# Reordering the head of a fused attention and GLU kernel: one load on ScalarE's queue, PSUM copies on ScalarE, late statistics on VectorE, and a GLU block moved ahead

## The chip, the cores and the metric

One core of a Trainium2 chip. The metric is the device time in microseconds. The profile of one execution gives the span from the first to the last instruction, about 1.7 us less than the time. The kernel before was timed on several chips beside the others; its medians there lie between 313.5 and 314.3 us, so each experiment is set against the runs of before on its own chip.

Six terms used throughout: a *block* is 128 rows of x (0 to 3 in the head), a *V half* is 320 of the 640 columns of V, *landing* is the moment the last of a load's 16 semaphore updates is recorded, the *q start* is the start of the first matmul of the q projection (everything before it is the *head*), the *chain* is the chain of waits that ended last, and the *granted clock* is the share of TensorE's full clock that the profile records. In the profile lines L600 is line 600 of that run's kernel. A chain line gives start, length, engine, tile and line; a timeline line gives start, busy time, engine, line, operation and tile, and in brackets how long the engine was idle before it and what ended that.

## The reference, cut to what matters

```python
xn = layernorm(x)                                    # x: 2048 x 640, bf16
qkv = xn @ wqkv                                      # 32 heads of 20, causal window of 256
a = softmax(mask(q @ k.T * 20 ** -0.5)) @ v @ wo
h = sigmoid(xn @ w_gate) * (xn @ w_up)               # 640 -> 1536
out = x + a + h @ w_down
```

## The kernel before: the parts that matter

The head loads x in four row blocks and V's weights in two halves, normalises each block, transposes it on TensorE and forms V before q and k. Engines run their instructions in the order in which they stand here.

```python
load_rows(0, nc.sync); load_rows(1, nc.sync)
load_v(0)                                            # first V half
load_rows(3, nc.sync); load_rows(2, nc.sync)
load_v(1)                                            # second V half
load_wqkv(0); load_wqkv(1)                           # q, k
...
for n in (6, 4):                                     # ten warming matmuls, 128x512 of ones
...
mv0 = ln_block(0, 0)                                 # VectorE: statistics of block 0
xn1, neg1 = mean_act(1)                              # ScalarE: mean of block 1
r0 = root(mv0)                                       # ScalarE: square root for block 0
r1 = root_act(1, xn1, neg1)                          # ScalarE: variance and root of block 1
norm(0, mv0, r0)                                     # VectorE
for lo, hi in ((0, 3), (3, DC)):
    transpose_rows(0, dve, lo, hi)                   # TensorE, then a copy out of PSUM
v00 = project_v(0, 0, 0)                             # TensorE: block 0, first V half
... # block 1, block 3 (its statistics on ScalarE), block 2
```

Much later the out projection of chunk 2 holds two PSUM banks open, and a GLU block of chunk 3 runs between its down sums and its wo sums:

```python
def g_out(c, between):
    for s in range(SBC):
        rows = new_rows(c, s)
        ys = [ps_d.tile([P, CW], FP32, name=f"y{i}", tag="d") for i in range(2)]
        for y, cut in zip(ys, HALVES):
            yield from down(c, s, y, cut)
        if s == 0:
            yield from between                       # one GLU block, two more banks
        outp(c, s, ys, rows)
```

The softmax here doesn't subtract the row's maximum and nothing guards it: scores larger than these inputs give would overflow.

## Time and profile before

| | before |
|---|---|
| time | 313.46 us median of 6 (313.23 to 315.04) |
| span of the profiled run | 311.6 us |
| TensorE busy | 304.0 us |
| first transposes on TensorE | 5.39 us |
| q start | 13.48 us |
| landings: block 1, first V half, block 3, block 2, second V half | 3.60, 5.90, 6.33, 6.78, 8.37 us |

TensorE is the bound, so the table is read by its first real work and by the q start. One profile is one execution: in another profile with the same head (e3) the second V half landed at 9.96 us and q started at 14.65, so differences of a microsecond between single profiles are not read as effects unless the waits in them show the cause. Landings are read from the semaphore records in the trace. The lines of the page and of the chain are shown in the prediction.

### The profile page before, as it was taken

The page shows a single profiled execution, that of the slowest core. Times are in us where ns is not written, and L with a number is a line of the kernel's source. Part 1 is how long each engine was busy: PE and PEld are TensorE (multiplying, and loading weights), DVE is VectorE, ACT ScalarE, POOL GpSimd, SP SyncE. Part 2 cuts the span into 40 slices and gives each one's busy share as a digit, 9 for nine tenths or more (in the row PEclk, how much of TensorE's full clock was granted, in tenths as well). Part 3 has the DMA queues.
Part 4 walks back from the last instruction along what each step waited for, and adds up shares of the span by engine and source line. Part 5 has one row for each costly group of instructions (what it writes and reads, how often), then busy time and mean ns, then how long its engine had stood idle before and what let it go on. Part 6 is the DMA issues. An engine that isn't in the chain of part 4 may idle for free.

```text
span 311.6 us, 10512 instructions
## 1 busy us (share of the span) xinstructions
PE 304.0 (98%) x4627; PEld 175.3 (56%) x4663; DVE 159.5 (51%) x314; ACT 192.4 (62%) x178; POOL 155.5 (50%) x239
## 2 busy tenths in 40 slices
PE   7999999999999999999999999999999999999996
PEld 2654444556557655644567665744556675444774
DVE  4633656639696164388826154362723526272523
ACT  6613878697763747787673647768585547778000
POOL 3000675676782828567382627546372845556000
PEclk9999999999999999999999999999999999999999
DMA  7995999574633153620025213730000223000002
GB/s 219 374 358 173 313 381 189 192 188 159 190 80 95 44 158 113 207 96 2 2 44 86 87 57 92 231 109 2 2 3 2 69 62 109 0 4 0 2 23 65
DMA packets 37614, 35.71 MB, mean 115 GB/s; under 512 B 10272, under 2 KB 37024, under 8 KB 37536
## 3 DMA queue, kind: packets, MB, share of 16 engines
q1 hardware_dynamic: 37280, 34.92, 37.8%
q8 instruction: 36, 0.59, 0.8%
q10 hardware_dynamic: 288, 0.11, 0.1%
q14 instruction: 10, 0.08, 0.1%
HBM read 23.63 MB, written 10.26 MB: 109 GB/s over the span
## 4 chain that ended last, share of the span: by engine, by line
PE 96%; issue 1%; DVE 1%; DMA 1%; ACT 0%; SPq 0%; DVEq 0%
PE y L421 17%; PE pu L407 17%; PE pg L400 17%; PE pqk L294 14%; PE ps L471 9%; PE pv L321 7%; PE y L428 7%; PE acc L503 7%; DMA xc<-in_A_x_dram 1%; PE pt L274 0%; DVE xnT L275 0%; ACT xn L598 0%; DVE h L411 0%; DVE xn L267 0%; SPq L171 0%
## 5 line engine op out<-in xcount | busy, mean ns | idle before, releaser
L479 POOL TENSOR_SCALAR_AFFINE_SELECT pT<-pT 128x512 bf16<-128x512 bf16 (+2 forms) x192 | 147.0, 796 | 129.2 <-ACT pT L476 129.1
L476 ACT ACTIVATE pT<-ps 128x2048 bf16<-128x2048 f32 x76 | 142.7, 1878 | 63.9 <-PE ps L471 59.2
L411 DVE SCALAR_TENSOR_TENSOR h<-th,pu 128x512 bf16<-128x512 f32 x48 | 32.7, 683 | 60.9 <-PE pu L407 49.2
L407 PE MATMUL pu<-xnT,wu 128*128 128x512 bf16 x228 | 59.2, 380 | 0.7
L400 PE MATMUL pg<-xnT,wg 128*128 128x512 bf16 x225 | 57.8, 380 | 1.0 <-issue 0.5
L421 PE MATMUL y<-wd,h 128*128 128x320 bf16 (+2 forms) x396 | 57.0, 296 | 0.0
L294 PE MATMUL pqk<-xnT,wqkv 128*128 128x512 bf16 x191 | 45.5, 381 | 0.5
L421 PEld LDWEIGHTS <-h 128*128 128x128 bf16 x396 | 36.5, 98 | 14.3
L403 ACT ACTIVATE th<-pg 128x512 f32<-128x512 f32 x48 | 28.6, 595 | 14.5 <-PE pg L400 14.0
L400 PEld LDWEIGHTS <-wg 128*128 128x128 bf16 x240 | 22.3, 98 | 25.3 <-issue 0.2
L407 PEld LDWEIGHTS <-wu 128*128 128x128 bf16 x240 | 21.9, 98 | 25.4 <-issue 0.6
L471 PEld LDWEIGHTS <-kT 20*64 20x64 bf16 x1856 | 20.6, 103 | 24.5 <-issue 22.6
L471 PE MATMUL ps<-qT,kT 20*64 20x128 bf16 (+4 forms) x1856 | 32.7, 239 | 0.1
L294 PEld LDWEIGHTS <-wqkv 128*128 128x128 bf16 x200 | 22.6, 119 | 18.0 <-issue 0.6
L432 DVE SCALAR_TENSOR_TENSOR rows<-y,rows 128x320 bf16<-128x320 f32 x30 | 14.5, 490 | 33.2 <-PE y L428 30.0
L513 DVE STREAM_TRANSPOSE t<-acc 128x512 f32<-128x512 f32 x32 | 22.0, 710 | 18.5 <-PE acc L503 18.2
L525 DVE TENSOR_TENSOR on<-t,rec 128x320 bf16<-128x320 f32 (+4 forms) x48 | 27.5, 573 | 1.1
L321 PE MATMUL pv<-wqkv,xnT 128*128 128x320 bf16 x160 | 23.6, 300 | 0.9 <-DVE xnT L275 0.9
L428 PE MATMUL y<-wo,oc 128*128 128x320 bf16 (+2 forms) x165 | 24.2, 295 | 0.0
L503 PE MATMUL acc<-pT,v 128*32 128x64 bf16 (+3 forms) x1376 | 23.2, 223 | 0.1
L503 PEld LDWEIGHTS <-v 128*32 128x32 bf16 x1376 | 18.6, 97 | 7.9 <-issue 1.9
L321 PEld LDWEIGHTS <-xnT 128*128 128x128 bf16 x160 | 14.9, 98 | 7.3 <-DVE xnT L275 1.3
(44 smaller groups left out, 132.6 us busy)
## 6 DMA issues: line engine op xcount, KB each, us to landing
qT<-sq SPq DMA_DIRECT2D x7, 512.0 KB, 5.6
sq<-st SPq DMA_DIRECT2D x20, 128.0 KB, 4.1
sk<-st SPq DMA_DIRECT2D x20, 128.0 KB, 3.0
rows<-in_A_x_dram SPq DMA_DIRECT2D x15, 160.0 KB, 2.4
out_dram<-rows SPq DMA_DIRECT2D x15, 160.0 KB, 1.8
kT<-sk SPq DMA_DIRECT2D x4, 512.0 KB, 6.1
wg<-in_B_w_gate_dram SPq DMA_DIRECT2D x2, 960.0 KB, 7.8
wu<-in_B_w_up_dram SPq DMA_DIRECT2D x2, 960.0 KB, 9.9
```

Of the source, the lines that this page charges most:

```text
L294: nc.tensor.matmul(ps, lhsT=wt[:, m, :], rhs=xnT[c][:, d, :], start=(d == 0), stop=(d == DC - 1))
L321: nc.tensor.matmul(ps[:, 0:HALF], lhsT=xnT[c][:, d, s * P:(s + 1) * P], rhs=wqkv[:, d, 2 * D + hf * HALF:2 * D + (hf + 1) * HALF], start=( ...
L400: nc.tensor.matmul(pg, lhsT=part(wg, d, f), rhs=xnT[c][:, d, :], start=(d == 0), stop=(d == DC - 1))
L403: nc.scalar.activation(out=th, in_=pg, func=TANH, scale=0.5)
L407: nc.tensor.matmul(pu, lhsT=part(wu, d, f), rhs=xnT[c][:, d, :], start=(d == 0), stop=(d == DC - 1))
L411: nc.vector.scalar_tensor_tensor(out=h, in0=th, scalar=1.0, in1=pu, op0=ADD, op1=MULT)
L421: nc.tensor.matmul(y[:, 0:cut[1] - cut[0]], lhsT=ht[c, f][:, s * P:(s + 1) * P], rhs=wd[:, f, cut[0]:cut[1]], start=(f == 0), stop=False)
L428: nc.tensor.matmul(y[:, 0:cut[1] - cut[0]], lhsT=oc[c, m][:, s * P:(s + 1) * P], rhs=wo[:, m, cut[0]:cut[1]], start=False, stop=(m == DC - 1))
L471: nc.tensor.matmul(ps[hf * U:(hf + 1) * U, i, col * U:(col + n) * U], lhsT=qk["k", kc, g // GH][32 * i:32 * i + DH, g % GH, key:key + U], ...
L476: nc.scalar.activation(out=pt[:, :, 0:CW], in_=ps, func=EXP, scale=SCALE)
L479: nc.gpsimd.affine_select(out=out, in_=in_, pattern=[[0, HG], [0, n], [sign, width]], compare_op=GE, fill=0.0, base=base, channel_multipli ...
L503: nc.tensor.matmul(acc[32 * i:32 * i + 32, q * U:(q + n) * U], lhsT=v[:, h * VW:h * VW + 32], rhs=pt[:, i, col * U:(col + n) * U], start=( ...
```

## The change

The second V half goes to ScalarE's queue, so that block 0 can form both V sums one after the other. The copies of blocks 0, 1 and 3 out of PSUM move to ScalarE, the statistics of block 3 to VectorE, the other order follows from that. The GLU block moves ahead of the down sums.

```diff
+    scr = const.tile([P, 1], FP32, name="scr")
+    nc.scalar.activation(out=scr, in_=nc.const_aps.tensor(1.0, [P, 1], FP32), func=SQRT)
-    load_v(1)
+    load_v(1, nc.scalar)
...
-            ys = [...]
+            if s == 0:
+                yield from ahead
+            ys = [...]
...
-    for lo, hi in ((0, 3), (3, DC)):
-        transpose_rows(0, dve, lo, hi)
-    v00 = project_v(0, 0, 0)
+    transpose_rows(0, act)
     norm_act(1, xn1, neg1, r1)
-    xn3, neg3 = mean_act(3)
-    r3 = root_act(3, xn3, neg3)
-    transpose_rows(1, dve)
+    transpose_rows(1, act)
+    v00 = project_v(0, 0, 0)
+    mv3 = ln_block(0, 3)
+    v01 = project_v(0, 0, 1)
+    r3 = root(mv3)
+    v10 = project_v(0, 1, 0)
+    norm(3, mv3, r3)
...  # block 3's copy on ScalarE, block 2's on VectorE, V copies in turns
-    fill.add("out2", g_out(2, g_gu(3, 0, 1)), OUT + GU)
+    fill.add("out2", g_out(2, (), g_gu(3, 0, 1)), OUT + GU)
```

More of the change, by code (lines that the diff above doesn't have):

```diff
@@ L171, in load_rows, with load_v @@
         queue.dma_start(out=xc[0][:, s, :], in_=xr[:, s, :])
-    def load_v(hf):
+    def load_v(hf, queue):
         a = 2 * D + hf * HALF
-        nc.sync.dma_start(out=wqkv[:, :, a:a + HALF], in_=wqkv_r[:, :, a:a + HALF])
+        queue.dma_start(out=wqkv[:, :, a:a + HALF], in_=wqkv_r[:, :, a:a + HALF])
     load_rows(0, nc.sync)
     load_rows(1, nc.sync)
-    load_v(0)
+    load_v(0, nc.sync)
     load_rows(3, nc.sync)
     load_rows(2, nc.sync)
-    load_v(1)
+    scr = const.tile([P, 1], FP32, name="scr")
+    nc.scalar.activation(out=scr, in_=nc.const_aps.tensor(1.0, [P, 1], FP32), func=SQRT)
+    load_v(1, nc.scalar)
     load_wqkv(0)
@@ L232 @@
     nc.gpsimd.memset(eps, EPS)
-    scr = const.tile([P, 1], FP32, name="scr")
-    nc.scalar.activation(out=scr, in_=eps, func=SQRT)
     for n in (6, 4):
@@ L450, in outp, with g_out @@
         store(c, s, rows)
-    def g_out(c, between):
+    def g_out(c, between, ahead=()):
         for s in range(SBC):
             rows = new_rows(c, s)
+            if s == 0:
+                yield from ahead
             ys = [ps_d.tile([P, CW], FP32, name=f"y{i}", tag="d") for i in range(2)]
@@ L621 @@
     norm(0, mv0, r0)
-    for lo, hi in ((0, 3), (3, DC)):
-        transpose_rows(0, dve, lo, hi)
+    transpose_rows(0, act)
+    norm_act(1, xn1, neg1, r1)
+    transpose_rows(1, act)
     v00 = project_v(0, 0, 0)
-    norm_act(1, xn1, neg1, r1)
-    xn3, neg3 = mean_act(3)
-    r3 = root_act(3, xn3, neg3)
-    transpose_rows(1, dve)
+    mv3 = ln_block(0, 3)
[3 more added lines that the diff above has]
+    norm(3, mv3, r3)
+    copy_v(0, 0, 0, v00, act)
     mv2 = ln_block(0, 2)
-    v10 = project_v(0, 1, 0)
-    copy_v(0, 0, 0, v00, act)
+    copy_v(0, 0, 1, v01, act)
+    transpose_rows(3, act)
+    v11 = project_v(0, 1, 1)
     r2 = root(mv2)
-    v01 = project_v(0, 0, 1)
-    norm_act(3, xn3, neg3, r3)
+    copy_v(0, 1, 0, v10, dve)
     norm(2, mv2, r2)
-    copy_v(0, 1, 0, v10, act)
-    transpose_rows(3, dve)
-    v11 = project_v(0, 1, 1)
-    copy_v(0, 0, 1, v01, act)
+    v30 = project_v(0, 3, 0)
+    copy_v(0, 1, 1, v11, act)
     transpose_rows(2, dve)
-    copy_v(0, 1, 1, v11, act)
-    proj_v(0, 3, 0, act)
-    proj_v(0, 3, 1, dve)
+    v31 = project_v(0, 3, 1)
+    copy_v(0, 3, 0, v30, act)
+    copy_v(0, 3, 1, v31, dve)
     proj_v(0, 2, 0, act)
```

## The prediction

> **What bounds the kernel now.** I read the page first, then the chain of waits, then the chain again for two short windows (the head, and the place where the GLU block moves), then the timeline of the head on all engines. From the page:
>
> ```profile
> PE 304.0 (98%) x4627; PEld 175.3 (56%) x4663; DVE 159.5 (51%) x314; ACT 192.4 (62%) x178; POOL 155.5 (50%) x239
> ...
> PE 96%; issue 1%; DVE 1%; DMA 1%; ACT 0%; SPq 0%; DVEq 0%
> ```
>
> The first line is busy time by engine over a span of 311.6 us, the second is the chain that ended last. TensorE is busy for 304.0 us and makes up 96% of the chain: nothing but TensorE's own idle time is left to save, 7.6 us in all. So I looked for where it idles. A list of its gaps from the trace shows only three over 0.2 us after the first matmul (0.51, 0.34, 0.59 us), all before 8 us. The rest are gaps of some 50 ns (single matmul records that are missing) and the time before the first and after the last matmul. The change works on the head, so here is the chain of waits for the first 16 us (start, length, what):
>
> ```profile
> 1.25 2.35 DMA xc<-in_A_x_dram
> ...
> 4.88 0.46 DVE xn L267
> 5.34 0.04 issue
> 5.39 0.36 PE pt L274 x3
> 5.74 0.02 issue
> 5.77 0.37 DVE xnT L275
> 6.13 0.05 issue
> 6.18 0.85 PE pv L321 x5
> 7.03 0.36 PE pt L274 x5
> 7.40 0.02 issue
> 7.42 0.50 DVE xnT L275
> 7.92 0.04 issue
> 7.97 1.53 PE pv L321 x10
> ```
>
> The path goes from one block's norm to its transposes on TensorE (L274), the copy out of PSUM (L275), its V matmuls (L321), then the next block's transposes and copy. From 9.5 us on it is TensorE alone. The projection of q starts at 13.48 us (timeline) and from there the chain is TensorE to the end, so **the start of the first q matmul, 13.48 us, is the figure through which the head moves the total**. From 5.39 to 13.48 us are 8.09 us. One V half is 5 matmuls, 0.136 us apart (2.72 us for 20 in the chain), so 0.68 us; five transposes issue in 0.28 us where they follow at once (10.48 to 10.76 us). 8 x 0.68 + 4 x 0.28 = 6.56 us of work, hence 1.53 us of waiting: that is all that the head's reordering can win.
>
> The second place, around 238 us:
>
> ```profile
> 236.95 1.09 PE pu L407 x5
> 238.05 0.03 issue
> 238.07 0.02 DVEq L411
> 238.09 0.04 issue
> 238.14 0.70 DVE h L411
> 238.84 0.04 issue
> 238.88 0.85 PE acc L503 x47
> ```
>
> Here a VectorE instruction is on the chain. PSUM has four banks in this pool; two hold the open sums y of the out block, two the GLU block's gate and up; the P.V sums of two groups then need two. The first takes the gate's, free early; the second waits until VectorE has read the up bank (h, 238.14 to 238.84).
>
> **What the Trainium skill says.** (1) "DMA: Bandwidth & Descriptors", Issuing engines are not separate DMA queues: loads begun by different engines run on the same 16 DMA engines and interleave; and Queues, rings and completion order: each engine takes turns between queues with work. This trace has only one loading queue in the head, so it can't show the turns; that the DMA engines are full it does show (share 0.61 before 5.39 us, about 1 from there to 24 us, in the windows). (2) "ScalarE: Activation LUTs", What ACT_TABLE_LOAD costs: 1283 ns for a table load (the trace: 1283), an ACTIVATE with immediates 186 + 0.833 ns per element (the trace: 736 ns at 640, the formula 719). (3) "VectorE: DVE Perf Modes", Why PSUM operands drop a tier: a PSUM source caps VectorE at two elements a cycle for bf16. The trace's copy of 128x640 took 492 ns; 640 elements at one per 0.96 GHz cycle would be 667 ns, so it agrees. (4) "TensorE: Matmul & The Clock Gate", What's actually happening: about 3.4 us of work opens the clock, an idle window of about 3.4 us closes it. The warming matmuls' weights are loaded 0.43 us apart, later 512-column matmuls run 0.215 us apart (50 from 13.48 to 24.22 us), which agrees; a pause under 1 us should not close it.
>
> **The change part by part, head.**
> - Start of ScalarE. Table load 0.80 to 2.08 us as before; the small square root no longer waits for GpSimd's eps (0.71 us idle now), so 2.28; the V load's issue, estimated 0.36 us as ScalarE's stores at the end take (0.34 and 0.37), ends at 2.65. Its first real work starts at 3.62 when row block 1 lands: hidden, costs nothing.
> - SyncE issues one load fewer (0.43 us), so q's and k's weights are asked for 0.45 us earlier. They land at 10.65 and 12.90 us (landings in the trace), needed from 13.48: hidden.
> - Copy of block 0 to xnT: VectorE did it in pieces of 357 and 280 ns, the first alone held up the V matmuls. Now one ScalarE copy: by ScalarE's own casts, 422 ns at 320 columns and 580 ns at 512, 0.82 ns each, estimated 0.69 us at 640. It runs 5.88 to 6.57, so xnT of block 0 is later by 0.24 us than its second piece was (6.33).
> - VectorE, freed of it, takes block 1's reciprocal at 5.82 and its norm until 6.46 (now until 6.88). TensorE does block 1's transposes 6.51 to 6.79, then three V sums without a break to 8.83, if V's halves are there. Copy 1 is done by 7.7, before it is needed at 8.15.
> - Statistics of blocks 3 and 2 on VectorE (0.88 + 0.21 us each, then a 0.29 us root on ScalarE, 0.15 reciprocal, 0.45 norm). With block 3 landed (6.33 us now) by 6.49: aggregate done 7.6, root 8.0, norm 8.65, transposes at 8.83 in time. ScalarE copies V00 and V01, then block 3's xnT 9.31 to 10.0; V11 runs to 9.79, V30 waits until 10.05 (0.26 us). Block 2's root comes after that copy in ScalarE's order: 10.29, norm 10.93, transposes at 10.98 (0.25 us waited), V31, then V20 at 12.0 after VectorE's copy, V21 to 13.37.
>
> So if every load comes in time q starts at about 13.4 us, **0.1 us earlier**: the waiting merely moves (0.84 us before block 1's transposes, 0.26, 0.25, 0.07).
>
> - The loads. V's second half is now asked for at 2.3 instead of 3.24 us and takes turns with the first half. The landings are now: first half 5.90, block 3 6.33, block 2 6.78, second half 8.37 us. The 0.4 MB of the second half took about 1.6 us after block 2. Moved ahead of the blocks it can delay both by up to that, and the first half too: with even turns both halves would land near 7.1, block 3 at 7.5, block 2 at 7.9. V00 then starts at 7.1 instead of 6.79, and block 3's statistics at 7.55 instead of 6.49. The same count gives block 3's transposes at 9.65, block 2's at 11.92, V21's end at 14.3: **0.8 us later**.
>
> **GLU block ahead.** The instruction order shows the ten gate and up matmuls moved before the first down sum and nothing else moved; the P.V sums now come after 24 down matmuls, with two banks long free. The first group's P.V starts at 237.96 and takes about 0.68 us, so the second could start at 238.64 and starts at 238.88: **0.24 us saved**.
>
> **Sum.** I weigh three cases for the head: in time (40%) -0.1 us, even turns with full delay (35%) +0.8 us, and better than my count (25%), with two queues filling the DMA engines, which moved only 180 GB/s on average before 5.39 us, and some copies shorter, -0.7 us: together about +0.1. With -0.24 for the GLU block: 313.98 + 0.1 - 0.24, about 313.8 us.
>
> **The rivals.**
> (a) *The second V half delays the row blocks* (a transfer takes the place of the wait removed). For it: full DMA engines from 5.39 us on; SyncE's single order had put blocks 3 and 2 ahead on purpose. Against: 180 GB/s before. The total would be about 314.5.
> (b) *ScalarE becomes the head's bound.* It has four copies or roots in strict order between 5.9 and 10.3 us, and block 2's root waits behind a copy it does not need. For it: ScalarE needs 0.69 where VectorE took 0.49 us. Against: VectorE no longer copies blocks 0, 1 and 3. It is in my count at 0.25 us; with a slower copy the total is 314.0 or so.
> (c) *All goes well*: V00, V01, V10 in one run, and TensorE loses only the first wait: q at 12.8 us, with the GLU block 313.0.
> (d) *A shift of the head changes later coincidences* of SyncE's q and k round trips with TensorE. The first scores start at 30.84 us with no gap on TensorE before them, so I expect the shift to carry through one to one; 0.2 us either way.
>
> **Range and chances.** The corners are 313.0 (c) and 314.5 (a); the three runs of before spread from 313.51 to 315.04, so a median of few runs adds some 0.3 us. Range 312.9 to 314.8. Two per cent is 6.3 us, four times all waiting in the head: faster 0.01, slower 0.005, the rest same.
>
> **What would show it.** The start of the first q matmul (13.4 in time, 14.3 with full delay, 12.8 at best); the landing of block 3, that is the start of the second pair of statistics on VectorE (6.5 or 7.5); TensorE's wait before the first V matmul; the ScalarE copy's duration (0.69); VectorE's h gone from the chain near 238 us and the 96 P.V matmuls there taking 1.52 instead of 1.77 us. I am wrong if q starts outside 12.8 to 14.3, if the move at the head does not reach the end, or if another stretch of TensorE changes by over 0.3 us.

## The result, and the profile after

The changed kernel took 316.21 us (median of 6, 315.93 to 317.06) where the one before took 313.46. The ratio is 1.0085, 95% interval 1.0061 to 1.011: slower by 0.85%, and outside the prediction's range (312.9 to 314.8). Ratios here are the mean time of one kernel's fast runs over that of the other's of the same rounds, so not quite the ratio of the medians.

The chain of the changed kernel, first 17 us (start, length, what):

```profile
1.25 3.71 DMA xc<-in_A_x_dram
4.96 0.02 issue
4.98 0.03 ACT xn L600
...
5.81 0.18 ACT rstd L590
6.00 0.82 ACT xn L605 x2
...
7.37 0.46 DVE xn L611
7.82 0.05 issue
7.87 0.71 PE pt L274 x5
8.58 3.32 PE pv L321 x15
11.90 0.29 PE pt L274 x5
...
16.41 0.22 PE pqk L294
```

Before, the chain waited for x until 3.60 us; now until 4.96. This load is block 1. From there ScalarE's statistics of block 1 are on the chain (L600, L605), then VectorE's norm of block 1 (L611). And 15 V matmuls take 3.32 us, where 20 took 2.72 us before. The timeline of the same kernel says why block 1 is late, and what it holds up:

```profile
0.80 1.28 ACT L183 ACT_TABLE_LOAD   x1 [0.80 <-PEq L770]
0.86 0.44 ACTq L175 DMA_DIRECT2D wqkv<-in_A_wqkv_dram  x1
2.09 0.20 ACT L183 ACTIVATE scr<-const-float32-1.0 128x1 f32<-128x1 f32 x1
4.98 0.74 ACT L600 ACTIVATE xn<-xc 128x640 bf16<-128x640 bf16 x1 [2.69 <-DMA xc<-in_A_x_dram]
5.72 0.28 ACT L590 ACTIVATE rstd<-mv,eps 128x1 f32<-128x1 f32 x1
6.73 0.45 PE L274 MATMUL pt<-ident,xn 128*128 128x128 bf16 x5 [1.91 <-DVE xn L267]
```

The second V half is issued at 0.86 us, *during* the table load behind which it stands in the program (0.80 to 2.08), and 0.39 us before block 1 (SyncE, 1.25). The small square root, which also stands ahead of it, ran only at 2.09. The V half lands at 4.49 and block 1 at 4.96 instead of 3.60. ScalarE then does block 1's mean (L600) ahead of block 0's root (L590), as the program says, so block 0, which landed at 3.25, also waits: its statistics are ready at 4.40, its root starts at 5.72. TensorE's first transposes start at 6.73 instead of 5.39.

The second loss is the clock. The windows of the changed kernel, four stretches of the head (length; busy us of each engine with its instructions; granted clock; DMA share; GB/s):

```profile
5.39:7.00 1.61, 0.27 (x5) 0.27 (x5) 0.61 (x2) 1.58 (x6) 0.00 (x0) 1.00 1.07 377
7.00:9.00 2.00, 1.31 (x12) 0.91 (x10) 1.61 (x5) 1.21 (x3) 0.00 (x0) 0.66 1.06 385
9.00:11.00 2.00, 2.00 (x9) 1.12 (x8) 1.40 (x4) 0.93 (x3) 0.00 (x0) 0.50 1.07 364
11.00:13.00 2.00, 1.89 (x17) 1.22 (x16) 0.70 (x2) 1.21 (x3) 0.00 (x0) 0.98 1.06 373
```

The granted clock was 0.50 from 7.65 to 11.06 us, one stretch of 3.41 us. In the stretch of that length before it (4.23 to 7.65) TensorE had been busy for only 1.04 us: it idled 1.91 us, and again from 7.18. In 9 to 11 us TensorE is fully busy with 9 V matmuls; before, the same window held 11 and ten transposes:

```profile
9.00:11.00 2.00, 1.99 (x21) 1.39 (x20) 1.49 (x5) 1.28 (x4) 0.00 (x0) 1.00 1.05 378
```

The q start moved from 13.48 to 16.25 us, 2.77 later: 1.34 before the first transposes and 1.43 after them. The span grew by 2.6. The GLU block did what was predicted; the chain near 240 us of the changed kernel has no VectorE step before the P.V sums (softmax weights times v, tile acc):

```profile
235.74 1.08 PE pu L407 x5
236.82 0.81 PE y L421 x6
237.63 0.36 PE ps L473 x32
237.99 2.55 PE y L421 x18
240.54 1.46 PE acc L505 x96
```

### The profile page after: what moved, and what is told of

Read it like the earlier page. It is cut to its first block, busy times and chain, and to the rows that moved or that the text cites.

```text
span 314.2 us, 10511 instructions
## 1 busy us (share of the span) xinstructions
PE 305.2 (97%) x4628; PEld 175.8 (56%) x4663; DVE 159.8 (51%) x314; ACT 192.1 (61%) x176; POOL 155.5 (49%) x239
## 4 chain that ended last, share of the span: by engine, by line
PE 96%; DMA 1%; issue 1%; ACT 1%; DVE 0%; SPq 0%
PE y L421 17%; PE pu L407 17%; PE pg L400 17%; PE pqk L294 14%; PE ps L473 9%; PE pv L321 7%; PE y L428 7%; PE acc L505 7%; DMA xc<-in_A_x_dram 1%; PE pt L274 0%; ACT xn L605 0%; ACT xnT L275 0%; DVE xn L611 0%; SPq L171 0%; ACT rstd L606 0%
## 5 line engine op out<-in xcount | busy, mean ns | idle before, releaser
L321 PE MATMUL pv<-wqkv,xnT 128*128 128x320 bf16 x160 | 25.0, 310 | 0.1
```

The lines of the kernel that those rows point to most:

```text
L321: nc.tensor.matmul(ps[:, 0:HALF], lhsT=xnT[c][:, d, s * P:(s + 1) * P], rhs=wqkv[:, d, 2 * D + hf * HALF:2 * D + (hf + 1) * HALF], start=( ...
```

## The experiments

Theory: the load on ScalarE's queue is issued too early, block 1 lands late, ScalarE's order hands the delay on to block 0, and the longer pause closes TensorE's clock. Rivals: the new order and the slower ScalarE copies lengthen the head; or a load on a second queue costs wherever it is issued.

**e1: the changed kernel with the load back on SyncE's queue.**

```diff
-    load_v(1, nc.scalar)
+    load_v(1, nc.sync)
```

> The changed kernel with one line undone: V's second half goes back to SyncE's queue, behind block 2's rows. My theory (the ScalarE-queue load is issued at 0.86 us, ahead of block 1's rows, and everything late in the head follows from it): block 1 lands at about 3.6 us again, TensorE's first transposes start at 5.4, the clock stays open, the first q matmul starts at 13.3 to 13.7 and the time is 313.0 to 313.6. Rival (the new order and the ScalarE copies, 0.69 us where VectorE took 0.49, make the head longer): q starts after 15 and the time stays over 315.

Block 1 landed at 3.61, the first transposes started at 5.41, q at 13.87. The ratio to before is 1.0007 (0.9976 to 1.0039): undoing one line takes back the loss. (One of its six runs, 317.16 us at a mean clock of 0.995, shows that the clock can close here too.) The q start is 0.2 us outside my range, because the second V sum waited for its half, which now landed at 7.96. The timeline of e1, TensorE:

```profile
6.84 0.84 PE L321 MATMUL pv<-wqkv,xnT 128*128 128x320 bf16 x5
...
8.00 1.52 PE L321 MATMUL pv<-wqkv,xnT 128*128 128x320 bf16 x10 [0.32 <-DMA wqkv<-in_A_wqkv_dram]
```

And its waits of TensorE after the head show a new one:

```profile
PE pu L407 <- DMA wu<-in_B_w_up_dram: 0.7, 1, 0.7
```

At 41.3 us TensorE waited 0.66 us for the second half of the up weights. In the kernel before that load landed at 40.08 and was first used at 40.14; in e1 it landed at 41.21. Its issue on SyncE's queue, in the timelines of before and of e1:

```profile
30.13 0.53 SPq L197 DMA_DIRECT2D wu<-in_B_w_up_dram  x1
31.44 0.53 SPq L199 DMA_DIRECT2D wu<-in_B_w_up_dram  x1
```

The issue came 1.31 us later where q started only 0.39 us later than before. My prediction said that a shift of the head carries through one to one, 0.2 us either way (rival d); here it did not. No profile here has a head earlier than before's 13.48 us, so what an earlier one would lose at this load is not shown.

**e2: the kernel before with the load part alone** (old order, no GLU block ahead).

```diff
-    load_v(1)
+    scr = const.tile([P, 1], FP32, name="scr")
+    nc.scalar.activation(out=scr, in_=nc.const_aps.tensor(1.0, [P, 1], FP32), func=SQRT)
+    load_v(1, nc.scalar)
...                                                  # the later square root of eps goes
```

> The kernel before with only the load part: V's second half on ScalarE's queue, with the early square root from a constant; old order, no GLU block ahead. My theory: the load alone does the harm, block 1 lands near 5.0 us, the first transposes start near 6.7, the first q matmul at 15 to 16.5, time 315 to 316.8. Rival (order and copies): equal to before, 313.2 to 314.0.

Ratio 1.0088 (1.0056 to 1.0119), the whole change's 1.0085: the load alone does the harm. Block 1 landed at 5.04 and the first transposes started at 6.81, as expected. In the profiled run the clock was at 0.50 for 6.83 us and q started at 17.50, later than I had said, and the median, 317.16, is over my range too. The three other runs, mean clock 0.995, took 316.1 to 318.5 us.

**e3: the kernel before with the GLU block ahead alone.**

```diff
-    fill.add("out2", g_out(2, g_gu(3, 0, 1)), OUT + GU)
+    fill.add("out2", g_out(2, (), g_gu(3, 0, 1)), OUT + GU)
```

> The kernel before with only the GLU block ahead. By the prediction's count 0.24 us less than before, about 313.2, with the 96 P.V matmuls near 238 us in 1.52 us instead of 1.77 and no VectorE step on the chain there. Rival: the wait only moves to a later bank, and the time is that of before within 0.1 us.

The 96 P.V matmuls took 1.52 us, nothing of VectorE on the chain there. The ratio, 0.9992 (0.9975 to 1.0008), agrees with the 0.24 us but can't be told from none. This profile also shows the weakness that the change was meant for. The second V half landed at 9.96 us, not 8.37 as in the first profile of before, and TensorE stood still for it:

```profile
10.00 0.85 PE L321 MATMUL pv<-wqkv,xnT 128*128 128x320 bf16 x5 [1.27 <-DMA wqkv<-in_A_wqkv_dram]
```

**e4: the changed kernel with 18 warming matmuls instead of 10.**

```diff
-    for n in (6, 4):
+    for n in (6, 12):
```

> The changed kernel with 18 instead of 10 warming matmuls, which fill TensorE's pause until about 6.6 us. My theory: the late load costs about 1.35 us of start and the closed clock another 1.3 us or so; with the pause filled the clock stays at 1.000, the first transposes still start at 6.7 to 6.8, 15 V matmuls take 2.2 us instead of 3.5, q starts at 14.7 to 15.0 and the time is 314.6 to 315.1. Rival (the clock hardly matters, the rest is waiting): q stays at 16 and the time at 316.0 to 316.3.

Block 1 still landed late (5.18) and the transposes started at 7.05, but the clock, once open at 5.54, stayed open. TensorE's timeline of e4:

```profile
7.05 0.44 PE L274 MATMUL pt<-ident,xn 128*128 128x128 bf16 x5
...
8.38 2.20 PE L321 MATMUL pv<-wqkv,xnT 128*128 128x320 bf16 x15
...
14.93 1.24 PE L294 MATMUL pqk<-xnT,wqkv 128*128 128x512 bf16 x5
```

Fifteen V matmuls took 2.20 us, against 3.53 in the changed kernel's timeline, so the closed clock cost the sum of 15 about 1.3 us, and q started at 14.93, as expected (the transposes started 0.25 us past what I had said). From first transposes to q it took 7.88 us, the changed kernel 9.52, the kernel before 8.09. The time, ratio 1.0027, is at the edge of what I expected; 0.85 us went to the up weights near 42.5 us.

**e5: the changed kernel again, unaltered.**

> The changed kernel again, unaltered, for its two clock states and on the same chip as the three below. Two of its six runs had a mean clock of 1.000 in the record and were still 1 us longer than the four with 0.995. My guess: in those the clock opened only after the head had begun (the record starts at the first opening), so that more of the head ran at half speed; a profile of such a run shows the first opening later than 5 us. Time 316 to 317.5, first q matmul at 16 or later. Rival: the 1.000 runs kept full speed and lost their time somewhere else.

Ratio 1.0080 (1.0046 to 1.0115) on another chip. The profiled run was of the 0.995 kind again (clock 0.50 from 7.93 to 11.35, q at 16.47), so it does not answer the question about the 1.000 kind; a profile of e7 does for that kernel. All twelve runs of the change, of either kind, took 315.9 us or more.

**e6: the load on ScalarE's queue, but behind block 1's mean in the program.**

```diff
-    load_v(1, nc.scalar)
...
     xn1, neg1 = mean_act(1)
+    load_v(1, nc.scalar)
```

> The changed kernel with the load of V's second half still on ScalarE's queue, but standing behind the mean of block 1 in ScalarE's program, whose wait for block 1's rows holds the issue back to about 3.6 us. My theory (the harm is the issue at 0.86, ahead of block 1's rows): block 1 lands at 3.6, transposes start at 5.4, q starts at 13.3 to 14.3, time 2 to 3 us below the changed kernel's on this chip. Rival (a load on a second queue is what costs, wherever it is issued): q stays over 15.

A miss by 6 us, and instructive. Half of it came as I said: the load was issued at 3.62, block 1 landed at 3.59, the transposes started at 5.37. But by then q's weights (SyncE, 3.23) were ahead and k's (3.71) beside it. The second V half landed at 12.25 us, after q's weights (10.34), and TensorE waited 4.66 us:

```profile
12.29 2.83 PE L320 MATMUL pv<-wqkv,xnT 128*128 128x320 bf16 x10 [4.66 <-DMA wqkv<-in_A_wqkv_dram]
```

The clock was at 0.50 from 11.29 to 18.12, too, and q started at 20.52. A second queue was no express lane here. I read it as the bytes that were asked for before it, but a q start after 15 is what the rival had named, and no run has this load at this time on SyncE's queue: e6 alone does not separate the two. Ratio 1.0197.

**e7: second V half on SyncE's queue, ahead of block 2.**

```diff
+    load_v(1, nc.sync)
     load_rows(2, nc.sync)
...
-    load_v(1, nc.scalar)
```

> The changed kernel with V's second half on SyncE's queue, but one place earlier than in e1, ahead of block 2's rows. In e1 the second V sum waited 0.3 us for that half. Expected: the half lands at about 7.5, block 2 at about 8.0 in time for its statistics at 8.5, q at 13.3 to 13.6. The total gains less: in e1 TensorE lost 0.66 us near 41 us to the second half of the up weights, and an earlier head loses more there. Time equal to e1's within 0.3, some 0.4 below before at most.

The half landed at 7.67, block 2 at 8.07, as planned, but the profiled run's q start was 15.21. TensorE's timeline:

```profile
4.63 0.63 PE L238 MATMUL pwarm<-const-bfloat16-1.0 128*128 128x512 bf16 x1
5.50 0.72 PE L274 MATMUL pt<-ident,xn 128*128 128x128 bf16 x5 [0.23 <-DVE xn L267]
...
7.15 3.72 PE L321 MATMUL pv<-wqkv,xnT 128*128 128x320 bf16 x15
```

The clock record of this run begins with an opening at 10.23 us: the warming matmuls never opened it, and V ran at half speed. This is how a run has a mean clock of 1.000 in the record and is still long. The record starts at the first opening. Its six runs fall apart in a way that fits, though only one of them was profiled: 313.0 twice, 314.0, and 314.9 three times. Ratio 0.9992 (0.9953 to 1.0032).

**e8: e7 with the second half of the gate and up weights in two pieces each, in turns.**

```diff
-        for t, w in ((wg, B_w_gate), (wu, B_w_up)):
-            nc.sync.dma_start(out=t[k], in_=...[:, :, k * FS:(k + 1) * FS])
+        n = 1 if k == 0 else 2
+        for a in range(0, FS, FS // n):
+            for t, w in ((wg, B_w_gate), (wu, B_w_up)):
+                nc.sync.dma_start(out=t[k][:, :, a:a + FS // n], in_=...)
```

> e7 with the second half of the gate and up weights loaded in two pieces each, gate and up in turns, so that the columns wanted first land first. If the wait near 41 us is for those columns, it goes (0 instead of 0.7 us or more) and the head's gain reaches the end: 0.8 to 1.2 us below before on this chip. Rival: the DMA engines are simply behind, the wait moves to the next block of columns, and the time is e7's.

q started at 13.69 and TensorE no longer waited near 41 us (no gap over 0.2 us there). The six runs lie between 312.9 and 313.5 us, ratio 0.9969 (0.9937 to 1.0001). The gain over before, 0.45 us by the medians, is less than the 0.8 I had hoped for, and the interval just takes in none. What the split itself gives is not shown: e7's two best runs, 313.04 and 313.05, lie within e8's range, and e8's profile has an open clock (from 5.80) where e7's had a closed one.

**e9: the changed kernel with block 0's root ahead of block 1's mean.**

```diff
-    xn1, neg1 = mean_act(1)
     r0 = root(mv0)
+    xn1, neg1 = mean_act(1)
```

> The changed kernel with its early load as it is, but block 0's square root ahead of block 1's mean in ScalarE's order. My theory: the late block 1 reaches block 0 only through ScalarE's order, so block 0's transposes start at 5.4 to 5.7 again; block 1's norm stays late (about 7.6) and TensorE does block 1's transposes ahead of the first V sum, so q still starts at 15 to 16.4 and the time falls by less than 1 us from the changed kernel's, to 315.3 to 316.3. Rival: block 0 itself is late for another reason; its transposes stay at 6.7.

Block 0's transposes started at 5.45 although block 1 still landed at 4.89: the delay had reached block 0 through ScalarE's order alone. It helped little, as TensorE then waited 1.85 us for block 1:

```profile
5.45 0.45 PE L274 MATMUL pt<-ident,xn 128*128 128x128 bf16 x5 [0.21 <-DVE xn L267]
7.76 0.45 PE L274 MATMUL pt<-ident,xn 128*128 128x128 bf16 x5 [1.85 <-DVE xn L611]
8.04 3.76 PE L321 MATMUL pv<-wqkv,xnT 128*128 128x320 bf16 x15
```

The pause moved and the clock closed all the same (0.50 from 8.50 to 11.91). Ratio 1.0059 (1.0039 to 1.0078).

**e10: e8 with block 1's rows on ScalarE's queue instead.**

```diff
-    load_rows(1, nc.sync)
+    load_rows(1, nc.scalar)
```

> e8 with block 1's rows issued from ScalarE's queue instead of SyncE's (a small load that is wanted early gets the early issue). Theory: loads are served in order of issue; the rows, issued at 0.86, still land behind block 0's at about 3.5, and SyncE's loads all go out 0.45 us earlier, so V's second half lands near 7.4 and the 0.17 us wait of the second V sum goes; q at 13.2 to 13.6, time as e8's or up to 0.4 below. Rival (turns between the queues): block 0's rows land late, at 3.4 or more, and the head is later.

The rival won: both blocks were issued at 0.80, and block 0 landed at 3.79 instead of 3.10, block 1 at 3.98. Block 0 came 0.69 us later, block 1 too came 0.46 later than e8's 3.52, though it was issued 0.45 earlier, and the first transposes started at 6.07 (e8: 5.39). The profiled run, 315.69 us, is the slowest of the 14 and one of two at a mean clock of 0.995 (0.50 from 7.84 to 11.25, q at 15.72), so its q start does not stand for the rest. Ratio 0.9997 (0.9984 to 1.0011).

**e11: e8 with the copies of blocks 0, 1 and 3 on VectorE.**

```diff
-    transpose_rows(0, act)   # and 1, and 3
+    transpose_rows(0, dve)
```

> e8 with the copies of blocks 0, 1 and 3 out of PSUM on VectorE again, the rest of the new order kept. The prediction called the ScalarE copies neutral (0.69 against 0.49 us, but VectorE free for the norms). Expected here: block 1's norm later by 0.4 us, as VectorE copies first, block 3's statistics and block 2's later too, q at 14.0 to 14.6, time 0.3 to 0.9 over e8's. Rival (ScalarE is the head's bound): q earlier than in e8 and the time below it.

q started at 15.15, later than I expected, with the V matmuls at full speed: VectorE's copy of block 0 (6.22 to 6.71) held up block 1's norm, and the whole row of statistics behind it: TensorE waited 1.14 us for block 1's norm, in e8 0.51. A little of it is the clock, which first opened at 6.07 (in e8 at 5.80): block 0's transposes took 0.71 us, in e8 0.63. Ratio 1.0012 (1.0001 to 1.0023), with five of the 22 runs at a mean clock of 0.995. So within the new order the copies seem better on ScalarE; e8 was not run beside it on this chip.

**e12: e8 with two dummy matmuls in the pause behind block 0's transposes.**

```diff
     transpose_rows(0, act)
+    ps = ps_d.tile([P, CW], FP32, name="pwarm", tag="d")
+    for k in range(2):
+        nc.tensor.matmul(ps[:, 0:256], lhsT=ones[:, 0:P], rhs=ones[:, 0:256], start=(k == 0), stop=(k == 1))
```

> e8 with two 256-column dummy matmuls in TensorE's pause between the transposes of blocks 0 and 1 (0.5 to 0.7 us idle there), to test whether that pause decides when the clock opens or closes. If it does, no run is above 314 us and the median is that of e8's good runs or below (0.6 to 1.0 under before on the same chip). Rival: the phase of the clock's window decides, whatever a 0.5 us pause holds; the spread stays as in e8 and e10, and the time is within 0.3 of e8's, 0.3 to 0.5 under before.

Median 313.33 of 14 runs against 313.99 of before on this chip, ratio 0.9984 (0.9969 to 0.9999). Two of the 14 runs were over 314 us, so the pause is not all of it, and no run of e8 stood beside it on this chip: what the two dummies give is left open (the profiled run had q at 13.99, after a wait of 0.46 us for the second V half). It is the fastest version whose interval lies clear of the kernel before, by 0.16%.

| run | what | median us | before, same chip | ratio to before |
|---|---|---|---|---|
| the change | all | 316.21 | 313.46 | 1.0085 |
| e2 | load alone | 317.16 | 314.30 | 1.0088 |
| e1 | all but the load | 313.97 | 314.30 | 1.0007 |
| e3 | GLU block alone | 314.11 | 314.30 | 0.9992 |
| e4 | all, more warming | 315.13 | 314.30 | 1.0027 |
| e5 | all, again | 316.40 | 313.67 | 1.0080 |
| e6 | load issued at 3.6 us | 320.35 | 313.67 | 1.0197 |
| e7 | load ahead of block 2 | 314.41 | 313.67 | 0.9992 |
| e8 | e7, gate and up in pieces | 313.22 | 313.67 | 0.9969 |
| e9 | all, block 0's root first | 316.08 | 314.05 | 1.0059 |
| e10 | e8, block 1 on ScalarE's queue | 313.90 | 314.05 | 0.9997 |
| e11 | e8, copies on VectorE | 314.50 | 314.05 | 1.0012 |
| e12 | e8, pause filled | 313.33 | 313.99 | 0.9984 |

## Why the prediction was wrong

**The step that failed is the first of its list, "Start of ScalarE".** It said that the V load's issue comes after the table load and the small square root, "ends at 2.65" and is "hidden, costs nothing". It was issued at 0.86 and ended at 1.29. I had read ScalarE's instruction order as an order in time. In the trace the load's issue stands on ScalarE's sequencer (ACTq), the table load on its engine (ACT), and the issue did not wait for the engine. Under "PSUM — Partial Sum Buffer", Engine vs sequencer instructions, the Trainium skill says that a sequencer instruction waits only until earlier instructions have been dispatched, not completed. That page speaks of a nop and was not one I looked up; this trace shows the same for a DMA issue, with 1.22 us between the issue and the end of the table load ahead of it.

The sum had started from 313.98 us, the median of the three runs then at hand, so the change's own effect was forecast at -0.14 us; measured from the median of six it was +2.75.

**The contention was foreseen, but on the wrong victim.** Rival (a) had the second V half delay blocks 3 and 2 and gave 314.5. With the issue at 0.86 it stood ahead of block 1, whose rows are wanted first: landing 4.96 for 3.60. Blocks 3 and 2 lost only 0.64 and 0.65 us (6.97 and 7.43). The two V halves did not take even turns to land "near 7.1": they landed at 4.49 and 6.54.

**ScalarE's order as a carrier was missed.** I counted ScalarE's order only between 5.9 and 10.3 us (rival b). That block 0's root stands behind block 1's mean cost nothing before, as block 1 was there in time. e9 shows that it alone made block 0 late.

**The clock.** "A pause under 1 us should not close it" was said of pauses of which one became 1.91 us. The clock closed for 3.41 us in both profiles of the change, and e4, which kept it open, got back about 1.3 us of V matmuls. The two terms, 1.34 us of late start and 1.43 us after it, make up the 2.77 us of the q start. The closed clock accounts for all of the second: with it open (e4) the stretch from the first transposes to q, 7.88 us, was 0.21 shorter than before's.

**When the clock closed.** The length of one pause does not tell it. Cut the first 20 us of all 14 profiles into stretches of 3.41 us, counted from the first opening: an open clock closed after the stretches in which TensorE was busy for 1.57 us or less (the change: 1.04) and stayed open after those with 2.05 or more (before: 2.18); a closed clock opened after those with 3.17 or more and not after those with 2.76 or less (e7's, from 3.41 to 6.82 us). These are busy times as the profile models them, one execution each. The kernel before has such runs too: on e5's chip two of eleven, 315.07 and 316.77 us, at mean clocks of 0.995 and 0.988.

**What held.** The ScalarE copy took 0.69 us as estimated. With the loads in time the new order is about neutral: by my count q was to start at 13.4, and e8, which lost 0.17 us to the V half, started it at 13.69, where the kernel before had 13.48 in one look and 14.65 in another (e3's, whose head is that of before). The GLU block's 0.24 us is in the trace (P.V 1.52 for 1.77 us), but no timing here resolves it. **What held in part:** the change's later head did reach the end (q 2.77 us later, the span 2.6, with the GLU block's gain in it). In e1 and e4, with q 0.39 and 1.45 us later than before, another 0.66 and 0.85 us went to the up weights near 41 and 42.5 us, which I had not looked at because no wait stood there before; rival (d) had allowed 0.2.

**Open:** how two queues share the DMA engines. In the change the early V half landed wholly before block 1; in e10 two loads issued together both slowed; in e6 the V half landed after the q weights issued 0.4 us earlier. None of these runs separates the order of issue from the size of the turns. That the phase of the clock's stretches makes the other long runs at a mean of 1.000 is not shown; only e7's profile caught such a run.

## What to carry to other kernels

In these runs a DMA issued from ScalarE's queue went out as soon as the sequencer reached it, at 0.86 us past a table load and a square root that had no wait, and at 3.62 us where an activation ahead of it waited for block 1 (e6). Where it stands in the program does not say when it starts: look at the issue in the timeline, and ask which earlier-wanted bytes it will stand ahead of. A wait that is free today (a root behind another block's mean, a load landing 0.06 us before its use) is where tomorrow's delay or gain will be lost. And before carrying a shift of the head through to the end, find the next load that TensorE needs and look at whether its issue moves by the same amount.

## What the Trainium skill lacked or had wrong

- "PSUM — Partial Sum Buffer", Engine vs sequencer instructions, tells of nops and semaphores only. A measured case of a DMA issue on ScalarE's queue that overtakes a running table load in the same way belongs there, in "DMA: Bandwidth & Descriptors" and in "Perfetto Trace Analysis", which tells in general how sequencer and engine run apart: issued at 0.86 us, during a table load that ran from 0.80 to 2.08. So does what held it back in e6: the issue, which has no wait of its own in the trace, started at 3.62 us together with the activation ahead of it that waited for block 1.
- "DMA: Bandwidth & Descriptors", Queues, rings and completion order, has each engine take turns between queues packet by packet. From this I worked out even turns for the two V halves. In the change the ScalarE queue's 0.4 MB, issued 0.39 us earlier, landed whole (4.49 us) before any of block 1's 16 updates on SyncE's queue (first at 4.60). The page lacks a measured example of how far a load runs ahead of a later one on another queue.
- "TensorE: Matmul & The Clock Gate", What's actually happening, gives the free-running window as about 3.4 us, and that agrees: the low stretches lasted 3.41 us, or 6.83, twice that. But it says that an idle window closes the clock, and here a stretch with 1.04 us of TensorE work in it was enough, and warming from 0.84 to 5.27 us did not open it in e7 (first opening 10.23 us; the stretch from 3.41 had 2.76 us of work in it, so no full window, which fits the page). How much of a window must be busy stands on no page that I read; here, at most 1.57 us closed it, 2.05 kept it open, 2.76 did not open it, 3.17 did.
- No page that I read says that the recorded mean clock leaves out what comes before the first opening: e7's profiled run has 1.000 and V matmuls 0.27 us apart (3.72 us for 15).
